# A fused attention, expert and GLU kernel: the second sequence's sinks, the unread products, and the places of weight splits, conversions and the token order

## The chip, the cores and the metric

The kernel runs on one core of a Trainium2 chip. The metric is the device time of one execution in microseconds (us). The names of the engines are those of the profile: PE (TensorE, products), DVE (VectorE), ACT (ScalarE), POOL (GpSimd) and SP (SyncE, which here only starts transfers). All work of an engine goes in the order in which it was written; the engines meet at semaphores. A number such as L133 is a line of the kernel before.

## The reference

Three layers follow each other on 2 sequences of 768 tokens, 512 wide: attention with 8 heads, in which a query sees the 128 keys up to its own position and the first 4 keys of its sequence (the sinks); a layer of 8 experts, where each token goes to the one expert with the largest logit, in the order of the tokens, and an expert takes at most `capacity` (384) of them; and a gated unit (GLU) on all tokens.

```python
scores = scale * np.matmul(q, k.transpose(0, 1, 3, 2))
keep = is_sink | in_window
a = np.exp(scores - max); a = a / (sum + 1e-09)
x = np.matmul(a, v)                           # 1536 tokens x 512

expert_idx = np.argmax(x @ w_gate, axis=1)    # disp[e, pos[i]] = x[i], pos counts up to capacity
h = np.maximum(np.einsum('ecd,edf->ecf', disp, w1), 0.0)
y = np.einsum('ecf,efd->ecd', h, w2)
out[i] = gate_w[i] * y[expert_idx[i], pos[i]]     # 0 for a token that found no place

gate = 1.0 / (1.0 + np.exp(-(x @ w_gate)))
val = x @ w_val
return gate * val @ w_out
```

## The kernel before

The program is one long list, written out by hand in the order in which each engine is to work; nothing reorders it. It has three stages.

**Products in parts.** A float32 operand is split into a high part (a cast to a rounded format) and a low part (the difference). A product then is three matmuls: high by high, low by high, high by low. So nearly everything exists twice: xh and xl (tokens), hh and hl (hidden values), yh and yl (expert results), gh and gl (gated values), and each weight block is a `pair`. The high part is made by ACT (a cast), the low part behind it by DVE (a subtraction). Expert weights are split by `split_w` (L132 on ACT, L133 on POOL in the attention and on DVE in the experts), after `load_w` (L125, SP) has brought the block into one of four `stage` buffers. GLU weights are converted by integer operations: `whole` (L150 on ACT, L151, L153 and L157 on DVE, for half a block each) and `convert` (L164 on ACT, L165 on DVE).

**Attention.** 24 half-steps n, two for each tile of 128 tokens (i = n // 2, a = n % 2); the second sequence begins at n = 12. A half-step computes scores for four heads (L277), their maxima (L285, DVE), exponentials (ACT), transposes, and the products with the values of the half-step two before. Between them stand, for earlier tiles, the gate's logits, the positions in the experts (L439 to L449) and the scatter of the token into its slot (POOL's indirect writes, L470). The sinks of a sequence are prepared once: `place_sinks` copies their values on POOL (L221, L222); `gate_sinks(b, 0)` makes 8 narrow products (L239) and ACT copies them beside the values (L243); `gate_sinks(b, 1)` casts the whole tile vsr to vsh (L246, DVE), and `gate_sinks(b, 2)` subtracts (L250, DVE). Ten weight splits are done on POOL in ten of the half-steps. `keep(n)` issues n products of ones that nobody reads (L494).

**Experts.** For each of 8 experts a tile of 128 tokens (xs) is transposed on PE (`turn_x`, L734), cast and subtracted (L737, L738), multiplied by the first layer (`products`, `go`, L763), put through `relu` (L767), transposed (`turn_h`, L773) and split (hh L776, hl L777), and multiplied by the second layer. `raw_y` copies the result out (L784, ACT), `put_y` transposes it (L793) and writes it into yh (L795, ACT) and yl (L796, DVE), where the tokens lie sorted by expert. An expert with more than 128 tokens has a second tile and one with more than 256 a third (xe); that is a branch (`more_tiles`, L855), decided by counts on the chip. With the data here the first and the last expert have three tiles, two others have two. Into the gaps go the splits of the next expert's weights (`split_next`), and in the last expert the conversions of the first GLU weights (`fills`). `order` computes where each token stands in the sorted list, and `order_ids` writes this list (idsd) by 12 indirect transfers from POOL (L693, two for each of the experts 1 to 6 in the program); `load_ids` reads it back on SP for the last stage.

**GLU.** 36 steps t, on columns of 512 sorted tokens. Each makes two products (`up`, L168 to L170), a sigmoid and a gating (L998 to L1000), gl (L1002, DVE), and the product with the output weights for the step before (`down`, into acc). DVE also converts the next weights. Results leave by indirect writes that use the token order (L1031).

Of the kernel before, what the change touches and what calls it, by code (L numbers as in the profile page):

```python
# [9 lines left out]
F32 = mybir.dt.float32  # L10
# [16 lines left out]
def kernel(  # L27
# [62 lines left out]
    base_k = const.tile([P, E], F32, name="base_k")  # L90
    base_d = const.tile([P, E], F32, name="base_d")
    ids = const.tile([P, NTILE], I32, name="ids")
    zeros = const.tile([P, 1], F32, name="zeros")
    zero = const.tile([P, DM], F32, name="zero")

# [77 lines left out]
    def attention():  # L173
        with ExitStack() as st:
# [388 lines left out]

            splits = [n for n in range(6, NQ) if n // 2 != NT][:AHEAD]
            for n in range(NQ):
                i, a = divmod(n, 2)
                if a == 0:
# [25 lines left out]
                if n >= 2:  # L595
                    pv(n - 2)
                    sink_pv(n - 2)
                if a == 0:
                    if i % NT == 1:
                        place_sinks(i // NT)  # L600
                    if i + 1 < NTILE:
                        place_v(i + 1)
                    if i >= 2:
                        for f in (logits, best, where, onehot):
                            f(i - 2)
                        gate(i - 2, 0)
                        gate(i - 2, 1)
                else:
                    gate_v(i)
                    keep(2)  # L610
                    if i % NT == 1:
                        for j in range(3):
                            gate_sinks(i // NT, j)
                    for j in range(2):
                        sink_gather(i, j)
                    if i >= 2:
                        place(i - 2)
                        gate(i - 2, 2)
                        scatter(i - 2)
# [18 lines left out]
            m = ps_s.tile([P, 512], F32, tag="s", name="m")[:, :E]  # L638
            nc.tensor.matmul(m, ones, acc[0], start=True, stop=False)
            nc.tensor.matmul(m, ones, oh_all[:, NTILE - 1], start=False, stop=True)  # L640
            keep(32)
            kd2 = sm.tile([P, 2, E], F32, tag="kd2", name="kd2")
            nc.vector.tensor_scalar(
                out=kd2[:, 0], in0=m, scalar1=float(cap), scalar2=None, op0=ALU.min
# [25 lines left out]
    def order(pool):  # L670
        def pick(base, name):
            t = pool.tile([P, NTILE, E], F32, tag="ot", name="ot")
            nc.vector.tensor_tensor(
                out=t, in0=oh_all, in1=base.unsqueeze(1).to_broadcast([P, NTILE, E]), op=ALU.mult
            )
            r = pool.tile([P, NTILE], F32, tag=name, name=name)
            nc.vector.tensor_reduce(out=r, in_=t, axis=AX.X, op=ALU.add)
            return r

        a = pick(base_k, "pk")  # L680
        d = pick(base_d, "pd")
        nc.vector.tensor_sub(out=d, in0=d, in1=a)
        nc.vector.scalar_tensor_tensor(
            out=d, in0=pos_all, scalar=float(cap), in1=d, op0=ALU.is_ge, op1=ALU.mult
        )
        nc.vector.tensor_tensor(out=a, in0=a, in1=pos_all, op=ALU.add)
        pi = const.tile([P, NTILE], I32, name="pi")
        nc.vector.tensor_tensor(out=pi, in0=a, in1=d, op=ALU.add)
        return pi

    def order_ids(pi, i0, i1):
        for i in range(i0, i1):
            nc.gpsimd.indirect_dma_start(  # L693
                out=idsd_v[i], out_offset=bass.IndirectOffsetOnAxis(ap=pi[:, i:i + 1], axis=0),
                in_=ids0[:, i:i + 1], in_offset=None, bounds_check=N - 1, oob_is_err=False,
            )
# [5 lines left out]
    def experts(yh, yl):  # L702
        with ExitStack() as st:
# [57 lines left out]
            def go(todo):  # L761
                for ps, a, b, start, stop in todo:
                    nc.tensor.matmul(ps, a, b, start=start, stop=stop)  # L763
# [37 lines left out]
            def zero_y(d):  # L801
                z = zeros.to_broadcast([P, YW])
                nc.vector.tensor_copy(out=yh[:, d], in_=z)
                nc.gpsimd.tensor_copy(out=yl[:, d], in_=z)

            def more_tiles(e, y, b, fills):


# [1 line left out]
                w1a, w1b, w2a, w2b = (weights(4 * e + x) for x in range(4))  # L810
                yr = raw_tile(0)

                def one(j, todo, cover):
                    todo = list(todo)
                    per = -(-len(todo) // 4)

                    def beside():
                        for f in todo[:per]:
                            f()
                        del todo[:per]  # L820

                    x = turn_x(xe[:, j - 1], 1)
                    go(cover[:4])
                    u = bank(ps_u, 1)
                    go(products(u, x, w1a, True, True))
                    beside()
                    ra = relu(u)
                    u = bank(ps_u, 1)
                    c = products(u, x, w1b, True, True)
                    go(c[:6])  # L830
                    ha = turn_h(ra, 0)
                    beside()
                    go(c[6:])
                    rb = relu(u)
                    beside()
                    yx = bank(ps_y, 1)
                    a = products(yx, ha, w2a, True, False)
                    go(a[:6])
                    hb = turn_h(rb, 2)
                    beside()  # L840
                    go(a[6:])
                    go(products(yx, hb, w2b, False, True))
                    r = raw_y(yx, raw_tile(1))
                    go(cover[4:])
                    put_y(e, j, r)

                def rest(todo):
                    for f in todo:
                        f()

                n = 4 * (len(fills) + 1) // 8
                with tc.If(cnt_e[e] > P) as more:
                    one(1, fills[:n], b)
                    raw_y(y, yr)
                    with tc.If(cnt_e[e] > 2 * P) as most:  # L855
                        one(2, fills[n:], [])
                    if fills:
                        with most.Else():
                            rest(fills[n:])
                with more.Else():  # L860
                    go(b)
                    raw_y(y, yr)
                    rest(fills)
                return yr

            V = nc.vector
            xs = {0: load_x(0), 1: load_x(1)}
            load_x_next = lambda e: xs.update({e: load_x(e)}) if e < E else None
            x = turn_x(xs[0], 0)
            yr, cnt_x, cnt_e = None, None, None  # L870
            for d in range(KD):
                zero_y(d)
            for e in range(E):
# [36 lines left out]
                if e:  # L910
                    split_next(m + 7, V)
                go(a[6:])
                if e:
                    split_next(m + 8, V)
                    split_next(m + 9, V)
                elif e == 0:
                    cnt_e = counts([nc.tensor.engine, nc.scalar.engine, nc.vector.engine])
                if e == 0:
                    pi = order(hp)
                elif e < 7:  # L920
                    order_ids(pi, 2 * (e - 1), 2 * e)
                fills = []
                if e + 1 == E:
                    for q in range(4):
                        fills += [partial(whole, q, h * 512, h * 512 + 512) for h in range(2)]
                        if q < 2:
                            fills.append(partial(convert, q))
                yr = more_tiles(e, y, products(y, hb, w2b, False, True), fills)
            load_glu(4, 0)
            load_glu(5, 1)  # L930
            load_ids()
            put_y(E - 1, 0, yr)
            for q in range(2, 4):
                convert(q)
                load_glu(q + 4, q)
# [10 lines left out]
    def glu(yh, yl):  # L946
        with ExitStack() as st:
# [105 lines left out]
            def run(t0, t1, w, half, before):  # L1053
# [6 lines left out]
                for t in range(t0, t1):  # L1060
# [9 lines left out]
                    for step in range(3):  # L1070
                        conv_a(parts, step)
                    g = up(n, r, w)
                    for x, h in pend:
                        conv_b(x % 4, todo[x][2], h * 512, h * 512 + 512, nc.vector)
                        if h and x + 4 < len(todo):
                            load_glu(todo[x + 4][1], x % 4)
# [138 lines left out]
```

## Time and profile before

| | |
|---|---|
| time, median of 3 runs | 638.82 us (633.33, 638.82, 640.81) |
| profiled execution | 642.39 us, its span 640.7 us |
| mean granted clock of PE | 0.977 |
| busy: PE, DVE, ACT, POOL | 94%, 56%, 48%, 17% of the span |
| attention, experts, GLU | to about 139, to about 351, to the end |

Times in rows are microseconds from the span's start. A row of the timeline gives the start, the time taken, the engine, the line, the operation with what it writes and reads, how many instructions of that kind stand behind each other, and in brackets how long the engine had stood before it and what it then got ("<-DVE hl L777": the subtraction on line 777). "issue" means that it waited for nothing that the profile shows. The granted clock is 1.00 at 2.4 GHz and 0.50 at 1.2 GHz.

### The profile page before, as it was taken

How to read it: one execution, taken by the hardware profiler on the slowest of the kernel's cores; microseconds unless marked ns; L12 is line 12 of the kernel's file. 1: busy time of each engine (PE TensorE's matmuls, PEld its weight loads, DVE VectorE, ACT ScalarE, POOL GpSimd, SP SyncE). 2: the span in 40 equal slices, each digit the busy share in tenths (PEclk: the TensorE clock that was granted, in tenths of full speed). 3: DMA queues.
4: the chain of work that ended last, by engine and by line, in shares of the span. 5: the costliest groups of instructions: out<-in, count | busy, mean ns of one | idle time of the engine just before them, and what ended most of it. 6: DMA issues, size and time to landing. Idle time of an engine off the chain costs nothing.

```text
span 640.7 us, 9351 instructions
## 1 busy us (share of the span) xinstructions
PE 605.1 (94%) x3324; PEld 501.4 (78%) x3324; DVE 360.8 (56%) x870; ACT 305.0 (48%) x590; POOL 106.9 (17%) x161
## 2 busy tenths in 40 slices
PE   9899989989799989999987999999999999999995
PEld 5888878957577767777765888888888888999994
DVE  2565556544118855828855999982218921238811
ACT  4678666612228856828744555552214521225411
POOL 3178676362500000000000000000200000200002
PEclk9999979999989999999997999999999999999999
DMA  8999956033007973936703555552101530103001
GB/s 186 318 282 327 292 157 203 17 119 132 0 2 248 330 279 103 334 124 205 289 11 123 197 196 198 193 180 88 65 1 66 197 131 1 65 1 98 35 1 70
DMA packets 43630, 93.97 MB, mean 147 GB/s; under 512 B 5664, under 2 KB 24352, under 8 KB 39728
## 3 DMA queue, kind: packets, MB, share of 16 engines
q1 hardware_dynamic: 39872, 86.24, 41.7%
q0 software_dynamic: 2304, 6.09, 2.5%
q10 hardware_dynamic: 1392, 0.86, 0.5%
q8 instruction: 34, 0.56, 0.4%
q14 instruction: 28, 0.23, 0.1%
HBM read 82.63 MB, written 10.75 MB: 146 GB/s over the span
## 4 chain that ended last, share of the span: by engine, by line
issue 44%; PE 6%; POOL 1%; DVE 1%; ACT 1%; DMA 1%; POOLq 0%; SPq 0%; DVEq 0%; ACTq 0%
PE u L763 5%; POOL out_dram L1031 1%; DMA ids<-idsd 1%; PE t L773 0%; ACT pair L132 0%; DVE stage L153 0%; ACT hh L776 0%; DVE hl L777 0%; PE t L734 0%; PE t L793 0%; POOLq L1209 0%; DVE pair L165 0%; ACT stage L150 0%; DVE stage L157 0%; DVE stage L151 0%
## 5 line engine op out<-in xcount | busy, mean ns | idle before, releaser
L168 PE MATMUL g<-yh,pair 128*128 128x512 f32 (+1 forms) x288 | 109.1, 379 | 1.3 <-ACT yh L795 1.3
L169 PE MATMUL g<-yl,pair 128*128 128x512 f32 (+1 forms) x288 | 109.1, 379 | 0.0
L170 PE MATMUL g<-yh,pair 128*128 128x512 f32 (+1 forms) x288 | 108.8, 378 | 0.0
L1031 POOL DMA_INDIRECT out_dram<-o,ids x11 | 10.8, 981 | 452.6 <-ACT o L1047 450.2
L1000 ACT CAST gh<-g 128x512 fp32r<-128x512 f32 (+1 forms) x36 | 21.4, 594 | 110.2 <-DVE g L999 106.2
L999 DVE TENSOR_TENSOR g<-g,g 128x512 f32<-128x512 f32 (+1 forms) x36 | 23.5, 652 | 84.4 <-PE g L170 84.4
L763 PE MATMUL u<-pair,xh 128*128 128x512 f32 x224 | 63.7, 413 | 6.7 <-ACT xh L737 5.8
L133 DVE TENSOR_TENSOR pair<-stage,pair 128x1024 fp32r<-128x1024 f32 x54 | 64.3, 1221 | 10.3 <-ACT pair L132 10.0
L132 ACT CAST pair<-stage 128x1024 fp32r<-128x1024 f32 x64 | 65.3, 1050 | 0.8 <-ACTq L855 0.8
L763 PE MATMUL u<-pair,hh 128*128 128x512 f32 x224 | 61.9, 403 | 1.5 <-ACT pair L132 1.5
L168 PEld LDWEIGHTS g<-yh,pair 128*128 128x128 f32 x288 | 54.5, 189 | 10.3 <-ACT yh L795 1.7
L169 PEld LDWEIGHTS g<-yl,pair 128*128 128x128 f32 x288 | 54.5, 189 | 8.6 <-issue 0.5
L170 PEld LDWEIGHTS g<-yh,pair 128*128 128x128 f32 x288 | 54.4, 189 | 7.7
L296 ACT ACTIVATE pt<-sc,neg 128x260 f32<-128x260 f32 (+1 forms) x96 | 44.6, 491 | 33.1 <-DVE neg L285 26.8
L763 PEld LDWEIGHTS u<-pair,xh 128*128 128x128 f32 x224 | 42.9, 198 | 17.8 <-ACT xh L737 7.6
L170 PE MATMUL acc<-pair,gl 128*128 128x512 f32 x132 | 51.5, 391 | 0.0
L169 PE MATMUL acc<-pair,gh 128*128 128x512 f32 x132 | 51.5, 390 | 0.0
L168 PE MATMUL acc<-pair,gh 128*128 128x512 f32 x132 | 51.4, 390 | 0.0
L763 PEld LDWEIGHTS u<-pair,hh 128*128 128x128 f32 x224 | 41.4, 190 | 12.2 <-issue 2.9
L998 ACT ACTIVATE g<-g 128x512 f32<-128x512 f32 (+1 forms) x36 | 20.5, 569 | 61.8 <-PE g L170 61.8
L331 PE MATMUL pv<-v,pts 128*128 128x73 f32 x352 | 42.3, 273 | 0.0
L331 PEld LDWEIGHTS pv<-v,pts 128*128 128x128 f32 x352 | 41.5, 193 | 0.0
(157 smaller groups left out, 1024.8 us busy)
## 6 DMA issues: line engine op xcount, KB each, us to landing
stage<-in_we_dram SPq DMA_DIRECT2D x64, 512.0 KB
stage<-in_wd_dram SPq DMA_DIRECT2D x30, 1024.0 KB
vraw<-in_vr_dram SPq DMA_DIRECT2D x11, 288.0 KB
kraw<-in_kd_dram SPq DMA_DIRECT2D x22, 132.0 KB
qraw<-in_qd_dram SPq DMA_DIRECT2D x22, 128.0 KB
vt<-in_vt_dram SPq DMA_DIRECT2D x11, 256.0 KB
slots<-zero SPq DMA_DIRECT2D x1, 2048.0 KB
xs<-slots SPq DMA_DIRECT2D x8, 256.0 KB
```

The source lines that it names most:

```text
L132: nc.scalar.copy(out=t[:, 0], in_=raw)
L133: eng.tensor_sub(out=t[:, 1], in0=raw, in1=t[:, 0].bitcast(F32))
L168: nc.tensor.matmul(ps, ah, bh, start=start, stop=False)
L169: nc.tensor.matmul(ps, ah, bl, start=False, stop=False)
L170: nc.tensor.matmul(ps, al, bh, start=False, stop=stop)
L296: nc.scalar.activation(out=pt_[i][:, h, :w], in_=scs_[n][j][:, :w], func=AF.Exp, scale=-1.0, bias=neg_[i][:, h:h + 1],)
L331: nc.tensor.matmul(pv_[n][:, h], pts_[n, h // 2][:, h % 2, j], vb[kb][:, 4 * a + h], start=(h == 0 and j == 0), stop=(h == 3 and j == len( ...
L763: nc.tensor.matmul(ps, a, b, start=start, stop=stop)
L998: nc.scalar.activation(out=g, in_=pss[0], func=AF.Sigmoid)
L999: nc.vector.tensor_tensor(out=g, in0=g, in1=pss[1], op=ALU.mult)
L1000: nc.scalar.copy(out=gh[:, :w], in_=g)
L1031: nc.gpsimd.indirect_dma_start(out=out_v[j], out_offset=bass.IndirectOffsetOnAxis(ap=ids[:, j:j + 1], axis=0), in_=o, in_offset=None, boun ...
```

## The change

It moves work; all results are computed as before.

- *Sinks.* In the second sequence `place_sinks` goes to n = 13 (before: 14) and `gate_sinks(1, 0)` to n = 14 (before: 15). The split of n = 15 goes to n = 18, and the load that followed it with it.
- *Unread products.* 36 instead of 32 before the experts, three behind the transposes of the first tokens (`fill_clock`), five before the first GLU product.
- *Token order.* `order` keeps its two last terms; the operation that adds them, and the 12 indirect writes, are issued in the GLU's step t = 2, and the list is read back at t = 6.
- *Middle experts.* The last two weight splits of an expert, and the loads behind them, went ahead of the branch; now they are `fills` of the second tile, or stand behind the last products where there is none, and their loads stand behind the branch.
- *Last expert.* The fills stand 2, 1 and 2 to a tile (before: 2, 2, 1 and none), each at another place. The first tile's result is copied out by DVE where there is a second tile, and put into yh and yl inside the branch.

```diff
+            splits = [n for n in range(6, NQ) if n // 2 != NT and n != 2 * NT + 3][:AHEAD]
...
+                if n == 2 or n == 2 * NT + 1:
+                    place_sinks(i // NT)
+                if n == 2 * NT + 2:
+                    gate_sinks(1, 0)
                 if a == 0:
-                    if i % NT == 1:
-                        place_sinks(i // NT)
...
-                        for j in range(3):
+                        for j in range(i // NT, 3):
                             gate_sinks(i // NT, j)
...
-            keep(32)
+            keep(36)
...
+    def order_ids():
+        nc.vector.tensor_tensor(out=pi, in0=pi_a, in1=pi_d, op=ALU.add)
+        for i in range(NTILE):
             nc.gpsimd.indirect_dma_start(
...
+            def fill_clock(n):
+                t = bank(ps_u, 1)
+                for _ in range(n):
+                    nc.tensor.matmul(t, ones, ones.unsqueeze(1).to_broadcast([P, 4, P]), start=True, stop=True)
...
                     go(products(u, x, w1a, True, True))
-                    beside()
+                    beside(2 if last else 1)
                     ra = relu(u)
...
                     ha = turn_h(ra, 0)
-                    beside()
+                    beside(1)
                     go(c[6:])
                     rb = relu(u)
-                    beside()
...
                     hb = turn_h(rb, 2)
-                    beside()
+                    beside(2)
...
                     r = raw_y(yx, raw_tile(1))
                     go(cover[4:])
+                    if cover:
+                        nc.vector.tensor_copy(out=yr, in_=y)
+                    elif last:
+                        put_y(e, 0, yr)
                     put_y(e, j, r)
...
                     one(1, fills[:n], b)
-                    raw_y(y, yr)
...
             x = turn_x(xs[0], 0)
+            fill_clock(3)
...
-                if e:
-                    split_next(m + 8, V)
-                    split_next(m + 9, V)
-                elif e == 0:
+                if e == 0:
                     cnt_e = counts([nc.tensor.engine, nc.scalar.engine, nc.vector.engine])
-                if e == 0:
-                    pi = order(hp)
-                elif e < 7:
-                    order_ids(pi, 2 * (e - 1), 2 * e)
-                fills = []
+                    order(hp)
+                fills = [partial(split_w, m + j, V) for j in (8, 9)] if 0 < e < E - 1 else []
...
+                if 0 < e < E - 1:
+                    load_w(m + 16)
+                    load_w(m + 17)
             load_glu(4, 0)
             load_glu(5, 1)
-            load_ids()
-            put_y(E - 1, 0, yr)
+            fill_clock(5)
...
                     g = up(n, r, w)
+                    if t == 2:
+                        order_ids()
+                    elif t == 6:
+                        load_ids()
```

The order on PE, before, at the turn from n = 14 to n = 15 (idle: an unread product; vst, wg_sb: the sinks' values and the gate's weights; s: scores):

```order
L494 MATMUL idle<-ones 128x512
L239 MATMUL m<-wg_sb,vst 96x16 x4
L439 LDWEIGHTS upper
L439 MATMUL m<-oh_all,upper 128x8
L441 LDWEIGHTS ones
L441 MATMUL m<-acc,ones 128x8
L277 MATMUL s<-kraw,qraw 128x132 x2
L277 MATMUL s<-kraw,qraw 128x128 x2
```

And in the change, where the products of the sinks (now L242) stand one block of scores (now L280) earlier:

```order
L280 MATMUL s<-kraw,qraw 128x128 x2
L313 MATMUL t<-ident,pt 128x128 x4
L334 MATMUL pv<-v,pts 128x73 x4
L242 MATMUL m<-wg_sb,vst 96x16 x4
L280 MATMUL s<-kraw,qraw 128x132 x2
```

Between them and the position counts (L439, now L442) a whole half-step of PE now lies, while DVE's cast of vsh keeps its place in DVE's own order.

The order on ACT, before, in a middle expert at the branch to its second tile (pair, stage: weights; t: transposed tokens or hidden values):

```order
L132 CAST pair_88<-stage_83 128x1024
L132 CAST pair_84<-stage_80 128x1024 x2
L852 COMPARE_AND_BRANCH
L737 CAST xh<-t 128x512
L767 ACTIVATE hr<-u 128x512
L776 CAST hh<-t 128x512
```

In the change:

```order
L135 CAST pair_91<-stage_86 128x1024
L866 COMPARE_AND_BRANCH
L741 CAST xh<-t 128x512
L135 CAST pair_87<-stage_83 128x1024
L771 ACTIVATE hr<-u 128x512
L780 CAST hh<-t 128x512
L135 CAST pair_87<-stage_83 128x1024
```

Two of the casts of weights that stood ahead of xh now stand behind it, one ahead of relu and one behind hh.

The order on DVE, before, in the last expert's third tile (L151, L153 and L157: a conversion):

```order
L738 TENSOR_TENSOR xl<-t,xh 128x512
L165 TENSOR_TENSOR pair_86<-stage_81,pair_86 128x512 x2
L151 TENSOR_SCALAR stage_82<-stage_82 128x512
L153 SCALAR_TENSOR_TENSOR stage_82<-stage_82 128x512
L157 SCALAR_TENSOR_TENSOR stage_82<-stage_82 128x512
L777 TENSOR_TENSOR hl<-t,hh 128x512
L151 TENSOR_SCALAR stage_82<-stage_82 128x512
L153 SCALAR_TENSOR_TENSOR stage_82<-stage_82 128x512
L157 SCALAR_TENSOR_TENSOR stage_82<-stage_82 128x512
L151 TENSOR_SCALAR stage_83<-stage_83 128x512
L153 SCALAR_TENSOR_TENSOR stage_83<-stage_83 128x512
L157 SCALAR_TENSOR_TENSOR stage_83<-stage_83 128x512
```

After these twelve rows a third conversion stands there before the second hl. In the change, from the first hl on:

```order
L781 TENSOR_TENSOR hl<-t,hh 128x512
L154 TENSOR_SCALAR stage_85<-stage_85 128x512
L156 SCALAR_TENSOR_TENSOR stage_85<-stage_85 128x512
L160 SCALAR_TENSOR_TENSOR stage_85<-stage_85 128x512
L781 TENSOR_TENSOR hl<-t,hh 128x512
L154 TENSOR_SCALAR stage_86<-stage_86 128x512
L156 SCALAR_TENSOR_TENSOR stage_86<-stage_86 128x512
L160 SCALAR_TENSOR_TENSOR stage_86<-stage_86 128x512
```

Of the three conversions between the first hl and the second, one is left; the two others stand behind the second hl.

## Rows read from the trace of the kernel before

**Rows 1.** The page's first part: busy time, share of the span, instructions of each engine.

```profile
PE 605.1 (94%) x3324; PEld 501.4 (78%) x3324; DVE 360.8 (56%) x870; ACT 305.0 (48%) x590; POOL 106.9 (17%) x161
```

**Rows 2.** PE's waits by what ended them: us in total, times, the longest.

```profile
PE u L763 <- ACT xh L737: 5.8, 5, 1.4
...
PE u L763 <- DVE hl L777: 3.2, 2, 2.1
```

**Rows 3.** Windows: the stretch, its length, PE's busy time, granted clock, DMA share, GB/s.

```profile
81.57:88.39 6.82, 3.99 (x24) 0.50 0.81 223
143.00:146.42 3.42, 3.42 (x10) 0.50 1.03 381
173.73:180.55 6.82, 5.95 (x14) 0.50 0.00 0
344.39:354.63 10.24, 8.20 (x23) 0.50 0.09 16
```

**Rows 4.** Timeline, the sinks of the first sequence (20.54) and of the second.

```profile
20.54 0.46 DVE L246 CAST vsh<-vsr 96x584 fp32r<-96x584 f32 x1 [2.92 <-ACT psk L352]
...
80.97 0.22 ACT L243 COPY vsr<-m 96x64 f32<-96x64 f32 x1
81.02 2.35 POOL L133 TENSOR_TENSOR pair<-stage,pair 128x1024 fp32r<-128x1024 f32 x1
...
81.29 2.40 DVE L246 CAST vsh<-vsr 96x584 fp32r<-96x584 f32 x1 [1.98 <-ACT vsr L243]
...
84.85 1.23 PE L277 MATMUL s<-kraw,qraw 64*128 64x132 f32 x6 [2.83 <-DVE pos_all L449]
```

**Rows 5.** Timeline, PE at the experts' begin.

```profile
132.81 7.07 PE L494 MATMUL idle<-ones 128*128 128x512 bf16 x32
...
140.70 0.63 PE L734 MATMUL t<-ident,xs 128*128 128x128 f32 x4 [0.82 <-DMA xs<-slots]
...
142.12 1.34 PE L763 MATMUL u<-pair,xh 128*128 128x512 f32 x4 [0.80 <-ACT xh L737]
```

**Rows 6.** Groups from 155 to 171, POOL: busy, mean ns, idle before.

```profile
L693 POOL DMA_INDIRECT idsd<-ids,pi x12 | 11.8, 984 | 15.2 <-DVE pi L688 11.8 <-issue 3.4
```

**Rows 7.** Timeline, the first expert, and in the last row the last one.

```profile
168.24 1.07 PE L763 MATMUL u<-pair,hh 128*128 128x512 f32 x4
...
169.97 0.98 POOL L693 DMA_INDIRECT idsd<-ids,pi  x1 [0.30 <-issue]
171.45 0.59 ACT L784 COPY yr<-u 128x512 f32<-128x512 f32 x1 [7.46 <-remote]
...
172.09 0.66 PE L793 MATMUL t<-ident,yr 128*128 128x128 f32 x4 [2.78 <-issue]
...
174.60 1.65 PE L763 MATMUL u<-pair,xh 128*128 128x512 f32 x3 [1.42 <-ACT xh L737]
...
327.40 0.59 ACT L784 COPY yr<-u 128x512 f32<-128x512 f32 x1 [4.92 <-PE u L763]
```

**Rows 8.** Timeline, PE in the first of the two middle experts with a second tile.

```profile
230.55 1.19 PE L763 MATMUL u<-pair,xh 128*128 128x512 f32 x4 [1.19 <-ACT xh L737]
...
232.37 1.19 PE L763 MATMUL u<-pair,xl 128*128 128x512 f32 x4 [0.63 <-DVE xl L738]
```

**Rows 9.** Timeline, PE in the last expert's third tile and at the GLU's begin.

```profile
331.27 1.20 PE L763 MATMUL u<-pair,xh 128*128 128x512 f32 x4 [1.22 <-ACT xh L737]
...
343.73 1.54 PE L763 MATMUL u<-pair,hl 128*128 128x512 f32 x4 [2.13 <-DVE hl L777]
...
347.71 1.97 PE L793 MATMUL t<-ident,yr 128*128 128x128 f32 x8 [0.73 <-ACT yr L784]
...
350.97 0.79 PE L168 MATMUL g<-yh,pair 128*128 128x512 f32 x1 [1.29 <-ACT yh L795]
```

**Rows 10.** Timeline, the ninth GLU step: gl on DVE, and the first product with the output weights.

```profile
427.33 0.69 DVE L1002 TENSOR_TENSOR gl<-g,gh 128x512 fp32r<-128x512 f32 x1 [0.69 <-ACT gh L1000]
...
429.18 0.39 PE L168 MATMUL acc<-pair,gh 128*128 128x512 f32 x1
```

More of the change, by code (lines that the diff above doesn't have):

```diff
@@ L92 @@
     ids = const.tile([P, NTILE], I32, name="ids")
+    pi_a = const.tile([P, NTILE], F32, name="pi_a")
+    pi_d = const.tile([P, NTILE], F32, name="pi_d")
+    pi = const.tile([P, NTILE], I32, name="pi")
     zeros = const.tile([P, 1], F32, name="zeros")
@@ L562, in attention @@
             nc.gpsimd.memset(zero, 0.0)
-            splits = [n for n in range(6, NQ) if n // 2 != NT][:AHEAD]
+            splits = [n for n in range(6, NQ) if n // 2 != NT and n != 2 * NT + 3][:AHEAD]
             for n in range(NQ):
@@ L683, in order @@
         nc.vector.scalar_tensor_tensor(
-            out=d, in0=pos_all, scalar=float(cap), in1=d, op0=ALU.is_ge, op1=ALU.mult
+            out=pi_d, in0=pos_all, scalar=float(cap), in1=d, op0=ALU.is_ge, op1=ALU.mult
         )
[L686 to L692, printed above, removed]
+        nc.vector.tensor_tensor(out=pi_a, in0=a, in1=pos_all, op=ALU.add)
+    def order_ids():
+        nc.vector.tensor_tensor(out=pi, in0=pi_a, in1=pi_d, op=ALU.add)
+        for i in range(NTILE):
             nc.gpsimd.indirect_dma_start(
@@ L811, in more_tiles, with beside @@
                 yr = raw_tile(0)
+                last = e + 1 == E
                 def one(j, todo, cover):
                     todo = list(todo)
-                    per = -(-len(todo) // 4)
-                    def beside():
-                        for f in todo[:per]:
+                    def beside(n):
+                        for f in todo[:n]:
                             f()
-                        del todo[:per]
+                        del todo[:n]
                     x = turn_x(xe[:, j - 1], 1)
@@ L849, in rest @@
                         f()
-                n = 4 * (len(fills) + 1) // 8
+                n = 5 if last else 2
                 with tc.If(cnt_e[e] > P) as more:
                     one(1, fills[:n], b)
-                    raw_y(y, yr)
                     with tc.If(cnt_e[e] > 2 * P) as most:
                         one(2, fills[n:], [])
-                    if fills:
+                    if last:
                         with most.Else():
                             rest(fills[n:])
+                            put_y(e, 0, yr)
                 with more.Else():
                     go(b)
-                    raw_y(y, yr)
-                    rest(fills)
+                    if last:
+                        raw_y(y, yr)
+                        put_y(e, 0, yr)
+                        rest(fills)
+                    else:
+                        rest(fills)
+                        raw_y(y, yr)
                 return yr
```

## The prediction

> **What bounds the kernel now.** I began with the busy times of the page: PE works 605.1 of the span's 640.7 us [rows 1], no other engine more than 56%. So the time is PE's, and since the change adds and removes hardly any product that counts, it can only win in two places: in the 35.6 us (640.7 - 605.1) in which PE stands, and where PE's clock is half. Second, the list of PE's waits by what ended them [rows 2]: the largest cause is a cast of transposed tokens (xh, 5.8 us in 5 waits), and a low part of hidden values (hl) holds it 3.2 us in 2. Third, the windows with the granted clock [rows 3]: apart from the tail there are four stretches at 0.50, that is 1.2 of 2.4 GHz, in which PE was busy 3.99, 3.42, 5.95 and 8.20 us. The same products take half of that at full clock, so these stretches cost 2.0, 1.7, 3.0 and 4.1 us, 10.8 together. Each lies at a cluster of waits. Fourth, the timeline around each stretch, which says which engine came late. The change touches all four places.
>
> **The change part by part.** Durations are of the one profiled execution: 642.4 us, 1.7 of it outside the span. It is 3.6 above the median of the three timed runs, 638.8, which spread from 633.3 to 640.8.
>
> A, *the sinks of the second sequence*. In the rows before [rows 4] ACT copies the gated sinks at 80.97, the cast to vsh on DVE follows at 81.29 and takes 2.40 us; the same cast in the first sequence took 0.46. What differs is POOL: its split runs from 81.02 to 83.37. Everything DVE owes the next scores is 1.9 us late and PE waits 2.83 at 84.85. With the gate products a step earlier, the cast no longer waits for ACT: DVE had stood for 1.98 us before it, so it can start at 79.3 and, at 0.46, end 1.2 us before the split starts. The 8 narrow gate products and ACT's 0.22 copy move with it, into a step without such a wait. The split of n = 15 goes to n = 18, which only changes when POOL is busy. Gain: 2.83 + 2.0 of clock = 4.8, of which I take 4.5 because other operands of those scores may be next. Bounds: 0 (the cast still meets the split) and 4.8.
>
> B, *the experts' begin*. Before [rows 5], 32 unread products end at 139.88 (132.81 + 7.07), PE waits 0.82 for the tokens (xs) and 0.80 for xh, and half clock follows. Each unread product takes 7.07 / 32 = 0.22: four more end at 140.76 and fill the first wait, the three behind the transposes (0.66) the second. Neither wait gets shorter; both are filled. Gain 1.7, the clock's price; bounds 1.7 and a loss of 0.1, if the last product ends after the tokens land.
>
> C, *the token order*. Before, POOL issues the 12 small indirect writes of idsd (0.98 us each, [rows 6]) in one run up to 170.95, in the first expert [rows 7]. In that time ACT's copy of the second tile's y is late: PE's last product before it ended at 169.31 and still the copy began at 171.45, half a microsecond after POOL's last issue. It waits for PE's semaphore alone, for a product eight further back. In the last expert the same copy, at 327.40, begins while those eight still run. PE then waits 2.78 (no releaser), and at 174.60 another 1.42 for xh, which stands behind two more copies on ACT; then the clock is half. In the change the writes are issued in the third GLU step, and one of those two copies goes to DVE. If the burst was what held the semaphore, the copy starts about 167.4, the transposes follow the products at 169.3, xh is there at about 171.05 and PE starts there instead of at 174.60: 3.55, and 3.0 of clock, 6.5, of which I take 6.3. If not, only the copy's 0.5 is won. Bounds 0.5 and 6.5; I take the upper one because POOL had no other work there and no other expert shows such a wait. The operation that turned the order into integers (0.17) leaves DVE here too.
>
> D, *the middle experts*. In the two that have a second tile, xh and then xl come 1.19 and 0.63 late [rows 8] (the other 1.18 and 0.61), since ACT and DVE finish two weight splits first. Now the splits stand behind the transposes' casts, where PE has twelve products to do per split. Of 3.6 us I take 2.8, as four products of cover are just enough for a cast of 0.6. Where there is no second tile ACT's order stays. The two weight loads moved behind the branch on SP serve splits far ahead, so I cost them at nothing; if that cover were gone, one split (about 1.1 us) would be waited for. Bounds 0 and 3.6.
>
> E, *the last expert*. The conversions of GLU weights stand ahead of hl on DVE, three in a row in the last tile: PE waits 2.13 at 343.73 and 1.1 (3.2 - 2.1, [rows 2]) in the tile before, 1.22 at 331.27 for xh, 0.73 at 347.71 for y's copy and 1.29 at 350.97 before the first GLU product [rows 9]. Now one conversion stands ahead of each hl, two are beside the second layer, the first tile's y is transposed while the third's is copied, and five unread products (1.1) fill the last wait. I take out 3.2 for hl, 0.5 of the 1.22 (the copy on ACT), 0.7 for the copy and 4.1 of clock: 8.5. I put back 1.5, for a conversion that still delays a cast and for the second GLU product, which needs yl some 0.5 after yh. Gain 7.0, bounds 3.2 and 8.5.
>
> F, *the GLU*. DVE delivers gl later against its use with each step: in the ninth it ends at 428.02 and PE's product starts at 429.18 [rows 10], 1.16 of slack. PE now loses no clock at the GLU's begin (some 1.7 us of its products there), DVE is no faster, so the slack falls to about -0.5; with the 0.17 operation moved in, PE stands 0.6 in all. The writes on POOL and the load on SP stand beside nothing that PE waits for, as long as they hold up no semaphore. Bounds 0 and a loss of 9 (rival 3).
>
> Sum: 4.5 + 1.7 + 6.3 + 2.8 + 7.0 - 0.6 = 21.7; 642.4 - 21.7 = 620.7, so **621 us**, 2.8% below the median. The stretches at half clock probably vary between runs, which would be why the runs of before differ; the kernel after should have few, so I don't take the 3.6 off again.
>
> **Rivals.** 1. The writes weren't what held the copy in the first expert (C gives 0.5): 626.5. For it: the burst runs for 15 us, and only one semaphore shows a delay. Against: the coincidence to half a microsecond. Chance 0.20.
>
> 2. The change doesn't hold the clock: narrow products and transposes stand for PE's work there, and the unread ones are too few, so that B's 1.7 and half of A's and E's 6.1 are lost: 620.7 + 4.8 = 625.5. For it: in the first stretch the clock is already half at 81.57, before PE stops. Against: through the 32 unread products of the experts' begin the clock stays full. Chance 0.12. The Trainium skill (TensorE: Matmul & The Clock Gate, Part 4: PE-mode transpose) says that a transpose doesn't count as PE's work in the same way; by that rule the end of the last expert, with 8 transposes, is the likeliest place for it.
>
> 3. The burst makes the same trouble in the GLU. One late semaphore of PE there, 4.1 us as in the first expert (167.4 to 171.45), less about 1 us of slack, stops PE 3 us, and if a stretch at half clock follows, 3 more: about 627. Chance 0.10.
>
> 4. Slower than before. DVE stands behind POOL as the cast did. That cast lost 1.94 us (2.40 - 0.46) to one operation of POOL [rows 4]; if each of the 12 issues costs DVE that, it is 23.3 us late with 1 us of slack, PE stands 22, and the sum is 643, more with half clock. It decides from 1.6 us each, (18.1 + 1) / 12, which brings it to the median. Against: an issue lasts 0.98, and what holds a port that long can cost 11.8 in all, which ends at 631.5. Chance 0.04. The Trainium skill (SBUF — State Buffer, Who interferes with whom) has the rule that speaks against this change: VectorE and GpSimd share a pair of ports as an exclusive lock, taken by casts and tensor_scalar, and POOL's descriptors are written through it. The cast's 2.40 agrees; no row here shows such an operation beside an issue. By the rule the writes belong where DVE rests, and the GLU's begin is where it doesn't.
>
> 5. The cast of the sinks still meets a split: 620.7 + 4.5 = 625.2. Chance 0.06, for POOL's split starts when the values before it land, and 1.2 us earlier is enough.
>
> **How the numbers follow.** The forecast has 0.48. All gains at their upper bounds and no stall in the GLU give 642.4 - 25.1 = 617.3; since before's own runs reach 5.5 below their median, I go to 613. Upwards, rivals 1, 2, 3 and 5 lie at 625 to 627, and two of them together at about 632. The range is 613 to 632. About 1% is what a measurement of this kernel can tell, 6.4 us. Below 632.4 lie the forecast and any one of rivals 1, 2, 3, 5, which makes 0.96; for two or three at once and terms that I misread I take 0.09 off: faster 0.87, same 0.08, slower 0.05.
>
> **What would show it.** A: the second cast of vsh at about 0.46, no wait near 84.8. B: full clock at the experts' begin with PE unbroken. C: the copy of y at the end of its product; a wait of over 2 us with no POOL work beside it would refute the burst. D: waits for xh under 0.5 in the two middle experts. E: the first GLU product some 22 us earlier than 350.97, at full clock. F: a few tenths before the first down product of steps seven to nine; several microseconds in the third or fourth step would be rivals 3 or 4. The forecast is wrong if a wait moves instead of going, above all in E, where DVE does the same work as before.

## The result: 0.8% faster, where 2.8% were forecast

The change takes 633.12 us (median of 20 runs), the kernel before 638.89 on the same occasion; the ratio is 0.9916, with a 95% interval of 0.9891 to 0.9941. So it is faster by 5.8 us where 18 were forecast against the median, and lies above the range; the interval is clear of 1, but the gain is under the 1% that the prediction took for what a measurement of this kernel can tell. The profiled execution took 641.88 us (span 639.8), one of the two slowest of the 20, so the sizes read from it are those of this one execution.

PE's waits in the profile after, as in [rows 2] (us in total, times, the longest):

```profile
PE acc L171 <- ACT gh L1016: 10.3, 3, 5.1
...
PE s L280 <- DVE pos_all L452: 1.5, 1, 1.5
...
PE u L767 <- ACT xh L741: 1.5, 2, 0.7
```

The waits for xh fell from 5.8 to 1.5 and those for hl are gone; the first row is new. The windows at half clock, as in [rows 3], the one ahead of the sinks and the tail left out:

```profile
87.39:97.63 10.24, 10.24 (x56) 0.50 0.34 111
384.35:387.76 3.41, 3.41 (x10) 0.50 1.47 260
408.24:415.07 6.83, 5.44 (x13) 0.50 0.85 274
```

The stretches at the experts' begin, in the first expert and at the turn from the last expert to the GLU are gone; the one behind the sinks is longer than before, and two in the GLU are new. The timeline of the stages that went as forecast answers to [rows 5], [rows 7], [rows 8] and [rows 9]:

```profile
137.28 7.93 PE L497 MATMUL idle<-ones 128*128 128x512 bf16 x36
145.08 0.63 PE L738 MATMUL t<-ident,xs 128*128 128x128 f32 x4
...
146.50 1.20 PE L767 MATMUL u<-pair,xh 128*128 128x512 f32 x4
...
170.06 0.59 ACT L788 COPY yr<-u 128x512 f32<-128x512 f32 x1 [3.55 <-PE u L767]
...
171.67 0.60 PE L797 MATMUL t<-ident,yr 128*128 128x128 f32 x4
...
173.43 1.21 PE L767 MATMUL u<-pair,xh 128*128 128x512 f32 x4 [0.73 <-ACT xh L741]
...
240.35 1.20 PE L767 MATMUL u<-pair,xh 128*128 128x512 f32 x4 [0.72 <-ACTq L868]
...
335.93 0.50 PE L171 MATMUL g<-yh,pair 128*128 128x512 f32 x1 [0.18 <-ACT yh L799]
336.75 0.47 PE L172 MATMUL g<-yl,pair 128*128 128x512 f32 x1 [0.32 <-DVE yl L800]
```

The copy of y starts while its products still run, no wait of PE in the experts is longer than 0.73, and the GLU's first product starts at 335.93, where it stood at 350.97 before. Fifteen microseconds were won by then. In this execution they are lost again in the GLU:

```profile
336.00:360.00 24.00, 23.68 (x104) 1.00 0.55 196
360.00:384.00 24.00, 21.14 (x93) 1.00 0.89 115
384.00:408.00 24.00, 18.22 (x70) 0.93 0.94 127
```

These are windows of 24 us (length, PE's busy time, clock, the share of time in which the DMA engines are busy, GB/s). From 360 on, when POOL issues the 12 writes of the token order, the DMA engines are busier (0.89 against 0.55) and move less (115 against 196 GB/s). The transfers' own view gives the time from issue to landing, first of 336 to 360, then of 360 to 412:

```profile
stage<-in_wd_dram SPq DMA_DIRECT2D x5, 1024.0 KB, 5.0
...
stage<-in_wd_dram SPq DMA_DIRECT2D x7, 1024.0 KB, 18.6
idsd<-ids,pi POOLq DMA_INDIRECT x12, 14.7
```

A block of GLU weights lands after 18.6 us instead of 5.0. Its 8 KB packets took 0.37 us each on the mean from 336 to 360 and 1.16 from 364 to 405, the longest 7.0. What follows in the timeline is the wait:

```profile
377.85 0.43 DVE L154 TENSOR_SCALAR stage<-stage 128x512 int32<-128x512 int32 x1 [4.32 <-DMA stage<-in_wd_dram]
377.91 0.70 ACT L153 ACTIVATE stage<-stage 128x512 f32<-128x512 f32 x1 [4.93 <-DMA stage<-in_wd_dram]
...
382.51 0.62 ACT L1016 CAST gh<-g 128x512 fp32r<-128x512 f32 x1 [3.42 <-DVE g L1015]
...
383.19 0.50 PE L171 MATMUL acc<-pair,gh 128*128 128x512 f32 x1 [2.86 <-ACT gh L1016]
...
409.63 0.80 PE L171 MATMUL acc<-pair,gh 128*128 128x512 f32 x1 [5.08 <-ACT gh L1016]
```

ACT's and DVE's parts of a conversion wait for the weights. The sigmoid stands behind ACT's part and is done at 379.09. The gating (L1015) stands behind seven operations of DVE's part, which last from 377.85 to 381.8; gh on ACT waits 3.42 for the gating, and PE waits for gh, three times, two of them with half clock beside or behind them. From the first GLU product to the last the GLU took 282.6 us before (350.97 to 633.6) and 297.1 after.

And at the sinks, answering to [rows 4]:

```profile
82.22 0.94 POOL L214 COPY v<-vraw 128x512 f32<-128x512 f32 x1 [2.14 <-DMA vraw<-in_vr_dram]
82.23 0.45 DVE L249 CAST vsh<-vsr 96x584 fp32r<-96x584 f32 x1
...
83.14 2.84 POOL L136 TENSOR_TENSOR pair<-stage,pair 128x1024 fp32r<-128x1024 f32 x1
...
84.26 1.76 DVE L358 TENSOR_TENSOR psk<-pt,psk 128x32 fp32r<-128x32 f32 x1 [0.49 <-ACT psk L355]
...
86.17 0.71 PE L280 MATMUL s<-kraw,qraw 64*128 64x132 f32 x6 [1.54 <-DVE pos_all L452]
```

The cast takes its 0.45, but POOL's split now meets the next subtraction on DVE (psk), which took 0.19 before and takes 1.76 here. The wait shrinks from 2.83 to 1.54, and the clock falls all the same.

### The profile page after: what moved, and what is told of

Its sections match the earlier page's. It is cut to its first block, busy times and chain, and to the rows that moved or that the text cites. A ratio compares the mean times of both kernels' runs of the same rounds, so it can differ in the third digit from the quotient of the medians.

```text
span 639.8 us, 9368 instructions
## 1 busy us (share of the span) xinstructions
PE 608.5 (95%) x3336; PEld 504.8 (79%) x3336; DVE 362.8 (57%) x874; ACT 303.5 (47%) x586; POOL 109.8 (17%) x161
## 4 chain that ended last, share of the span: by engine, by line
issue 70%; PE 12%; DMA 6%; ACT 4%; DVE 3%; POOL 3%; POOLq 0%; SPq 0%; ACTq 0%; DVEq 0%
PE pv L334 4%; DMA idsd<-ids,pi 3%; PE s L280 2%; PE t L313 2%; ACT pt L299 2%; PE m L231 1%; ACT pts L321 1%; POOL idsd L697 1%; DMA ids<-idsd 1%; DMA vt<-in_vt_dram 1%; POOL out_dram L1047 1%; PE idle L497 1%; PE pv L372 1%; POOL yl L808 1%; DVE x L389 1%
## 5 line engine op out<-in xcount | busy, mean ns | idle before, releaser
L1015 DVE TENSOR_TENSOR g<-g,g 128x512 f32<-128x512 f32 (+1 forms) x36 | 23.4, 650 | 84.8 <-PE g L173 84.8
L767 PE MATMUL u<-pair,xh 128*128 128x512 f32 x224 | 60.7, 398 | 3.1 <-ACT xh L741 1.5
L171 PE MATMUL acc<-pair,gh 128*128 128x512 f32 x132 | 53.4, 405 | 10.3 <-ACT gh L1016 10.3
L173 PE MATMUL acc<-pair,gl 128*128 128x512 f32 x132 | 53.3, 404 | 0.0
L172 PE MATMUL acc<-pair,gh 128*128 128x512 f32 x132 | 53.2, 403 | 0.0
L697 POOL DMA_INDIRECT idsd<-ids,pi x12 | 14.2, 1182 | 224.2 <-DVE pi L695 214.3
L767 PEld LDWEIGHTS u<-pair,xh 128*128 128x128 f32 x224 | 40.8, 188 | 13.1 <-ACT xh L741 3.1
L334 PE MATMUL pv<-v,pts 128*128 128x73 f32 x352 | 45.0, 283 | 0.0
```

The source lines that it names most:

```text
L171: nc.tensor.matmul(ps, ah, bh, start=start, stop=False)
L172: nc.tensor.matmul(ps, ah, bl, start=False, stop=False)
L173: nc.tensor.matmul(ps, al, bh, start=False, stop=stop)
L334: nc.tensor.matmul(pv_[n][:, h], pts_[n, h // 2][:, h % 2, j], vb[kb][:, 4 * a + h], start=(h == 0 and j == 0), stop=(h == 3 and j == len( ...
L697: nc.gpsimd.indirect_dma_start(out=idsd_v[i], out_offset=bass.IndirectOffsetOnAxis(ap=pi[:, i:i + 1], axis=0), in_=ids0[:, i:i + 1], in_of ...
L1015: nc.vector.tensor_tensor(out=g, in0=g, in1=pss[1], op=ALU.mult)
```

## The experiments

Each ratio is to the kernel before on the same chip, with its interval. Chips differ: the kernel before took 636 to 643 us.

**The token order back in the first expert, alone in the kernel before, left out, and spread.**

```diff
 x1_order_back, from the change
-                    if t == 2:
-                        order_ids()
-                    elif t == 6:
-                        load_ids()
...
                     order(hp)
+                    order_ids()
...
             load_glu(5, 1)
+            load_ids()
 x2_order_only: the kernel before, with the first four lines added, the writes and the reading back at their old places taken out
 x3_no_order: the change, with nc.vector.tensor_copy(out=ids, in_=ids0) at t == 2 instead
 x4_order_spread: the change, with order_ids(2 * t - 4, 2 * t - 2) at t = 2 to 7, load_ids() at t == 10
```

> The change, with the token order as before: the 12 indirect writes in the first expert, the list read back before the GLU. Theory 1 (the writes hold up the GLU's weight loads): the three waits for gh (10.3 us) and the half clock behind them go; in the first expert the wait of about 2.8 us comes back, with half clock; about 633 - 14 + 6 = 625 us. Theory 2 (the GLU's weights are late because the GLU now begins 15 us sooner, writes or not): the waits in the GLU stay, about 633 us or more.

> The kernel before, with the token order alone moved into the GLU (writes at step 2, read at step 6). Theory 1: the waits for the GLU weights appear although the GLU begins as late as before, about 10 us and half clock; the 2.8 us wait of the first expert goes; about 639 - 6 + 12 = 645 us. Theory 2: no new wait in the GLU, 633 us.

> The change, with the 12 writes and the reading back left out (the list is a copy of the tokens' own numbers, so the rows of the output stand in another order). Theory 1: no wait for gh in the GLU and none in the first expert, 633 - 14 = 619 us. Theory 2: the waits in the GLU stay, 633 us.

> The change, with two writes in each of the GLU's steps 2 to 7 instead of 12 in step 2, and the reading back at step 10. Theory 1, with the hold-up in proportion to the writes pending at a time: each step's loads are late by less than their lead, 620 to 625 us. Theory 1, with the hold-up the same as long as any write is pending: loads late in six steps, 633 us or more. Theory 2: 633 us.

Without the token order, in x3 and later in y4, z1 and z4, the rows of the output stand in another order.

Measured: x1 626.02 (0.9695, 0.9629 to 0.9761), x2 645.84 (1.002, 0.9978 to 1.0062), x3 621.85 (0.9643, 0.9588 to 0.9698), x4 631.72 (0.9803, 0.9742 to 0.9864). With the writes out of the GLU the waits for gh are gone in x1 and x3 although the GLU begins at 336.07 and 339.45, far ahead of 350.97, so theory 2 falls. Put into the kernel before, the writes bring such waits (two, 3.8 us) although its GLU begins late, at 351.79, and eat what the first expert gains. Spreading them keeps the trouble: x4 is 5.7 us over x1; the waits of x4, then of x1:

```profile
PE acc L171 <- ACT gh L1017: 10.0, 3, 9.1
```

```profile
PE u L767 <- ACT xh L741: 2.3, 2, 1.5
PE t L797 <- issue: 2.0, 1, 2.0
PE s L280 <- DVE pos_all L452: 1.5, 1, 1.5
```

x1 has C's wait back. x4 had none at the sinks: there POOL copied the values (vraw) 2.2 us behind the cast of vsh (80.39 and 78.23) and not beside it as in the change (82.22 and 82.23), so its split began after psk, and the kernel reached the experts at 135.3 instead of 140.7.

**The order before the experts, POOL's split moved away from the sinks, and plain writes.**

```diff
 y1_order_early, from x1: order(hp) and the sum go ahead of turn_x(xs[0], 0), order_ids() behind the zero fill of yl
 y2_split_later, from x1; y5_early_split, from y1
-            splits = [n for n in range(6, NQ) if n // 2 != NT and n != 2 * NT + 3][:AHEAD]
+            splits = [n for n in range(6, NQ) if n // 2 != NT and n // 2 != NT + 1][:AHEAD]
 y4_direct_writes, from x3
+                        for i in range(NTILE):
+                            nc.gpsimd.dma_start(out=idsd[i * P:(i + 1) * P, :], in_=ids0[:, i:i + 1])
```

> The change, with the order computed before the first expert's first transposes and the 12 writes issued on POOL behind its zero fill of yl, at about 144 to 159, when no weights are loaded; the list is read back before the GLU. If the writes only cost where loads or a copy meet them, there is no wait in the GLU and none of 2 us at the first expert's third tile: 642.7 x 0.9643 = 620 us on the chip of the first runs, as without the writes. If a run of writes always holds up one of PE's semaphores by 4 us, a wait appears in the first expert's first or second tile: 624 to 626 us, as with the order as before.

> The change with the token order as before (x1_order_back), and POOL's split of n = 14 moved to n = 19 too, so that no split runs while DVE prepares the sinks. If POOL's split is what lengthens the cast or the subtraction of the sinks' scores (2.40 and 1.76 us against 0.46 and 0.19), the wait at about 84 us and the half clock behind it go whenever the values land: 2 to 5 us under x1_order_back, ratio 0.962 to 0.966. If the wait has another cause, 0.9695 again.

> The change without the token order (as x3_no_order, the rows of the output stand in another order), but with 12 plain writes of the same size (128 times 4 bytes each, to consecutive places) issued by POOL in the GLU's step 2. If small writes in flight hold up the weights, the waits in the GLU are back: 629 to 633 us. If it takes the indirect form, 621 us as without them.

> Both at once: the order early (y1_order_early) and the split of n = 14 moved (y2_split_later). If both causes are right, this is the fastest: ratio to the kernel before about 0.957 to 0.961, some 615 us on the chip of the first runs. If the early writes hold something up, it equals y2_split_later.

Measured: y1 624.07 (0.98, 0.9756 to 0.9843), y2 616.95 (0.9727, 0.9677 to 0.9777), y4 623.94 (0.9814, 0.9773 to 0.9855), y5 619.71 (0.9746, 0.9708 to 0.9784). y2's profile has no wait of PE over 0.75 from the sinks to the last chunk, and nothing at 0.50 before 610. The ratio doesn't show it: it is above the expected 0.962 to 0.966 and no lower than x1's, on another chip. The profiles do. Of the six with the sinks moved and the split in its place (the change, x1, x3, x4, y1, y4) all but x4 wait 1.5 to 2.0 at the second sinks, with half clock there (in y4 the split meets the subtraction L253, 2.79 instead of 0.76); of the seven with the split moved too (y2, y5 and later z1, z2, z4, w1, y6) none does, and none has half clock there. So the split was the cause; y1 and y5, which differ by it alone and ran on one chip, are some 4 us apart. y1 and y5 missed: neither has a late copy, but both wait 1.7 us for xl, and y5's timeline says why:

```profile
135.39 6.17 POOL L807 CAST yl<-zeros 128x1664 fp32r<-128x1664 f32 x4 [1.78 <-issue]
...
137.11 0.25 DVE L683 TENSOR_REDUCE pk<-ot 128x12 f32<-128x96 f32 x1
137.28 1.33 DVE L679 TENSOR_TENSOR ot<-oh_all,base_d 128x96 f32<-128x96 bf16 x1
...
138.93 1.13 DVE L688 TENSOR_TENSOR pd<-pd,pk 128x12 f32<-128x12 f32 x1
```

An operation of 12 columns takes 1.13 beside POOL's casts, the reduction 0.25. y4 didn't answer its question: its writes depended on nothing of the GLU and were issued at 142 to 161, where they held up the tokens of the second tile by 2.4 us.

**Bounds, a repetition, the split alone, and plain writes in the GLU.**

```diff
 z1_split_no_order: x3 with y2's line. z2_again: y2. z3_split_only: the kernel before with y2's line
 z4_plain_writes, from z1
+                        nc.vector.tensor_tensor(out=pi, in0=pi_a, in1=pi_d, op=ALU.add)
+                        for i in range(NTILE):
+                            nc.gpsimd.dma_start(out=idsd[i * P:(i + 1) * P, :], in_=pi[:, i:i + 1])
```

> As y2_split_later, but without the 12 writes and the reading back (the rows of the output stand in another order). It bounds what the token order costs where it stood before. If the writes in the first expert hold up the copy of y each time, it is 4 to 6 us faster than z2_again in all runs; if only in some runs, the two have the same fastest runs and z2_again some slower ones.

> y2_split_later once more, beside z1_split_no_order on the same chip: about 0.9727 of the kernel before. A second profile of it tells whether the copy of y in the first expert is late (as before and in x1_order_back) or not (as in y2_split_later) under the same instructions.

> The kernel before, with POOL's splits of n = 14 and 15 moved to n = 18 and 19 and nothing else. If POOL's split is the whole cause of the 2.40 us cast, the cast takes 0.46, the wait of 2.83 shrinks to about 0.9, and with the clock that follows the kernel gains 2 to 5 us, ratio 0.992 to 0.997, without the sinks moved at all. If the sinks' place is what matters, ratio 1.00.

> As z1_split_no_order, with 12 plain writes of the token order's size (128 times 4 bytes, consecutive places) issued by POOL in the GLU's step 2; they take their data from the operation of that step, so they can't go earlier as in y4_direct_writes. If small writes in flight hold up the weight loads, 10 us over z1_split_no_order and packets of weights of several us; if it takes the indirect form, within 1 us of it.

Measured, on one chip: z1 616.25 (0.9612, 0.9573 to 0.965), z2 622.61 (0.9719, 0.9676 to 0.9763), z3 641.09 (0.9978, 0.9944 to 1.0012), z4 624.74 (0.9746, 0.9704 to 0.9789). z4 is 8.5 us over z1, and its wait for gh, with the windows of the GLU (350 to 374 holds the writes), has the marks of the change:

```profile
PE acc L171 <- ACT gh L1016: 5.1, 1, 5.1
```

```profile
326.00:350.00 24.00, 23.68 (x104) 1.00 0.54 194
350.00:374.00 24.00, 20.21 (x90) 0.97 0.87 129
```

So it doesn't take the indirect form: 12 writes of 512 bytes, in pieces of 4, are enough. z4 doesn't read the list back, so it doesn't take that either. z2 against z1 is what the token order costs in the first expert: 6.4 us on this chip, and every run of z2 is slower than every run of z1. The copy of y is late in z2 and was in time in y2, under the same instructions; both rows follow, z2's first:

```profile
164.24 0.59 ACT L788 COPY yr<-u 128x512 f32<-128x512 f32 x1 [6.66 <-PE u L767]
164.88 0.66 PE L797 MATMUL t<-ident,yr 128*128 128x128 f32 x4 [1.97 <-issue]
```

```profile
160.83 0.59 ACT L788 COPY yr<-u 128x512 f32<-128x512 f32 x1 [3.55 <-PE u L767]
```

z3 shows that the split alone isn't enough: the cast is back at 0.46, but DVE still stands 1.98 ahead of it for ACT's copy of the sinks, as in [rows 4]; PE waits 1.04, and still runs the next 10 us at half clock, so the gain isn't told from none.

```profile
82.22 1.23 PE L277 MATMUL s<-kraw,qraw 64*128 64x132 f32 x6 [1.04 <-DVE pos_all L449]
```

```profile
81.98:92.22 10.24, 10.00 (x53) 0.50 0.36 89
```

**The failed step by itself, and a version that keeps the rest.**

```diff
 w1_change_split: the change with y2's line
 y6_order_behind, from y5: DVE's order operations behind turn_x(xs[0], 0), not ahead of it
```

> The change as it is, with POOL's split of n = 14 moved to n = 19 and nothing else. Without the varying wait at the sinks it differs from z1_split_no_order (0.9612) by the token order in the GLU alone. If small writes in flight are what the change lost its gain to, it lies 10 to 14 us above: ratio 0.977 to 0.984, with waits of 5 to 10 us in the GLU behind weight loads. If the gain was lost at the sinks, 0.962 to 0.966.

> The early order of y5_early_split with DVE's operations on it behind the subtraction of the first tokens, not ahead of it, where POOL's zero fill made them 1.1 to 1.7 us each. If that was the wait of 1.7 us, and a copy of y is late only when writes are in flight at its time, no wait is left before the GLU or in it: 0.960 to 0.963, as without the token order. If early writes hold up the loads of the second and third tiles' tokens, a wait of 2 us at the second tile: 0.966 to 0.970.

Measured, on one chip: w1 626.24 (0.9846, 0.9795 to 0.9897), y6 617.85 (0.9714, 0.9669 to 0.9758). The two differ by 8.4 us, all of it in the GLU: it begins at 326.9 and 326.7 and takes 289.7 and 281.3 us from first to last product. It takes 281.2 to 281.3 in all nine kernels with the change's other parts and no writes in the GLU (x1, x3, y1, y2, y4, y5, y6, z1, z2), and 288.7 (z4), 289.7 (w1), 296.1 (x4) and 297.1 (the change) with them. Windows of w1, then of y6:

```profile
351.00:375.00 24.00, 21.75 (x94) 0.97 0.88 119
375.00:399.00 24.00, 21.65 (x84) 0.88 0.80 197
```

```profile
351.00:375.00 24.00, 24.00 (x108) 1.00 0.55 195
375.00:399.00 24.00, 24.00 (x108) 1.00 0.46 163
```

In y6 the writes go out at 141 to 157, behind the loads of the tokens and before the copy of y. No wait over 0.75 is left from the sinks to the last chunk. It computes all that the kernel before does and is 18.8 us under the kernel before on its chip, 8.4 under the change with the same split. By ratio it isn't told from x1, y2 and z2, but its six runs lie within 2.6 us and its profile has no late copy.

The expected ratios of y1, y2, y5, y6 and w1 came from chips on which the kernel before took 642 to 643, and all five were missed, w1's barely. Ratios don't carry from chip to chip here: y2, z1 and y6 took 617, 616 and 618 us on three chips on which the kernel before took 636, 642 and 637. The kernels' differences on one chip are the firmer number.

## Why the prediction was wrong

The step that failed is F: "The writes on POOL and the load on SP stand beside nothing that PE waits for, as long as they hold up no semaphore." They stand beside the loads of the GLU weights, which PE does wait for, through the conversions on ACT and DVE and the gating behind them. I had counted the writes as 12 issues on POOL and one semaphore, not as traffic on the 16 DMA engines that the weights use. The row that would have said so was in the page of the kernel before (GB/s in 40 slices of 16 us):

```profile
GB/s 186 318 282 327 292 157 203 17 119 132 0 2 248 330 279 103 334 124 205 289 11 123 197 196 198 193 180 88 65 1 66 197 131 1 65 1 98 35 1 70
```

The DMA engines move 193 to 198 GB/s in the GLU's first four slices (352 to 416), and 0 and 2 from 160 to 192, around the place where the writes stood before (156 to 171). F was priced at -0.6, for gl late on DVE; no such wait is in the profiles without the writes (x1, x3, z1). The writes cost 8.4 us (w1 against y6), and 15.8 in the one profile of the change (297.1 against 281.3). Rival 3 had the place and about the size (6 us), but another mechanism, a late semaphore of PE; rival 4's port didn't decide: POOL's issues there took up to 1.51 instead of 0.98, and of DVE's operations only the shift of the conversion (L154) took longer, up to 0.59 instead of 0.43. Why so few bytes slow the loads so much isn't shown.

The median lies 12.4 us above the forecast. F explains 7.8 of it, by w1 and y6. The largest candidate for the rest is A, which won nothing in the change's profile: w1, the change with the split moved, took 626.24, but on another chip, so that this part isn't shown within one chip.

- *A, 4.5.* Right in y2 and x4 (experts reached 5 us sooner), wrong in the change's own profile, where nothing was won. I had followed the cast alone out of POOL's way and not the subtraction behind it; whether that meets the split hangs on when POOL gets the values (vraw), beside the cast in the change and 2.2 us behind it, so that the split comes after psk, in x4. Rival 5 named the collision, with the wrong operation. The Trainium skill (SBUF — State Buffer, Who interferes with whom) says that a VectorE instruction with two SBUF inputs contends with a GpSimd instruction that reads SBUF; psk at 1.76 against 0.19, and the 12-column operation at 1.13, agree, and a reduction beside the same cast stays at 0.25.
- *B, 1.7.* Right: from the first transposes of xs to the second tile's 12.7 us before and 11.1 after, at full clock.
- *C, 6.3.* Right in size, 6.4 (z2 against z1), where the copy is late; y2's profile, in which it isn't, is only 0.6 longer than z1's. That the burst is the cause is only half shown. The copy is late in four of the five profiles in which POOL was issuing writes at its time (before, x1, z2, z3; not y2) and in none of the other eleven, though in three of those (y1, y5, y6) the last writes had been issued only 3.5 to 5.3 us ahead and, by the 8 us that they take there, had not landed. So it goes with the issuing, if with the writes at all. The coincidence that the prediction leaned on, a copy half a microsecond after POOL's last issue, didn't repeat: in x1, z2 and z3 the copy starts 0.2 to 0.3 before that issue ends. How the copy comes late stays open.
- *D, 2.8.* Right in kind, larger: from the second tile of one of these experts to that of the next 42.1 us before, 40.1 after, and from there to the last expert's 42.2 and 40.2, so 4.0 for both.
- *E, 7.0.* Right, larger: 38.9 us from the last expert's second tile to the GLU before, 31.7 after, and 1.4 of clock behind it (the GLU's 282.6 before against 281.3), 8.5. The waits for hl didn't move; they went. Rival 2 fell: the end of the last expert, with its transposes, ran at 1.00 in the change's profile.

The terms before the GLU, A in its good case, make 26 us where I had 22.3; z1, with the split moved and no token order, is 26.2 under the kernel before.

## What to carry to other kernels

A transfer that is moved takes its traffic with it: look at what the DMA engines carry at the new place, and at who waits for that, as closely as at the queue that issues it; bytes say nothing, for 6 KB in pieces of 4 bytes cost a kernel 8 us. Operations on VectorE with two inputs in SBUF and GpSimd's work on SBUF belong apart, and when one of them is taken out of the way, the next in the queue is to be checked too. A stretch without loads that are waited for is the place for scattered writes, as in y6; in y4, at about the same place, a load of tokens came late beside them.

## What the hardware showed

- Small writes in flight slow the loads beside them: blocks of 1 MB landed after 18.6 us instead of 5.0 (13.5 in w1), packets of 8 KB took 1.16 us on the mean and up to 7.0 (8.0 in z4) instead of 0.37 and 1.37. The 12 writes themselves took 14.7 us from issue to landing (13.4 in w1), and 7.9 in y6, where they ran beside few loads. The Trainium skill (DMA: Bandwidth & Descriptors, Issuing engines are not separate DMA queues) states that transfers from all issuing engines run on the same 16 DMA engines and interleave, which agrees: the weights go out on SP and the writes on POOL.
- DVE operations of 12 columns that need 0.17 us (z1) take 1.13 and 1.48 beside a cast on POOL (y5), and psk, of 32 columns, 1.76 beside a split. In the change psk ends at 86.02 and the split at 85.98, so that it ended with POOL's.
- The same program ran at 617 us on one chip and 622 on another (y2 and z2); their profiles come apart by the late copy and the half clock behind it, 4.9 us at the GLU's begin.
